# x of one half folded into two accumulators mid-pair; weights' low parts on VectorE at the change of pairs; the opening's last chunk in a scores bank

## The chip, the cores and the metric

The kernel runs on one core of one Trainium2 chip. The metric is the time of one execution on the device, in microseconds (us); of several executions the median is taken. Beside the plain runs there is one profiled execution, whose trace gives the start and length of every instruction on the core's engines: TensorE (PE, with its weight loads PEld), VectorE (DVE), ScalarE (ACT), GpSimd (POOL), and SyncE's queue (SP), which issues nearly all transfers.

## What is computed

One transformer block with adaptive layer norm: sliding attention over a cache, and a gated feed-forward part. Cut to what matters:

```python
mod = (_silu(c) @ w_mod).reshape(c.shape[0], 6, 1, -1)
sa, ca, ga, sb, cb, gb = ...
h = _layernorm(x) * (1 + ca) + sa
x = x + ga * attention(h, k_cache, v_cache, wq, wo)   # 32 query heads, 16 kv heads, Dh 128, last 512 keys
h = _layernorm(x) * (1 + cb) + sb
g, u = h @ w_gate, h @ w_up                           # 576 -> 4608
x = x + gb * ((sigmoid(g) * u) @ w_down)              # 4608 -> 576
```

S = 2048 rows, D = 576, F = 4608, all in float32. The result is x.

## The kernel before

The 2048 rows are four **blocks** of 512 (NB = 4), of four tiles of 128. A float32 product is made of three matmuls on a high and a low part of each operand (`three`): the high part is a rounded copy that ScalarE makes, the low part is the difference, which VectorE or GpSimd makes.

**The opening and the attention.** Blocks 0 and 1 are normalised first. Their normalised rows are transposed in five chunks of channels (NC = 4 whole ones, and the tail as the fifth, k = 4) into the operand hTm (tail: hTt); `ln_shifted` reads a chunk's PSUM bank twice, ScalarE for the high part and then VectorE for the low part. For block 1 `chunks1` does this between the first steps of attention (chunks 0 and 1 in one step, 2, 3 and 4 in the next): even chunks in a bank of the tag ot (two banks, one of which holds the running sum of P times V), odd ones in the only bank wo. Scores and the transposes of exp(scores) take turns in four banks of the tag st. The next step's projections of q (qp<-hTm) follow on TensorE.

**The feed-forward part** uses Strassen's scheme (Winograd's form, seven products in place of eight) twice: blocks are taken in **pairs** (0: blocks 0 and 1; 1: blocks 2 and 3). The loop `for u in range(U + 1)` goes through 72 **units**, one group of 128 hidden channels each: NF = 36 for pair 0 (u = 0 to 35), 36 for pair 1. A unit has seven `product`s of seven matmuls in the banks a (two), b and c; the last of a unit, A22, runs in the next unit, behind that unit's A11. v1 is the running value that takes the last sum from a bank a (DVE v<-a,v) before A22 may add to that bank.

In a product's course `downs` places one or two steps of the second matmul (`down_some`: three matmuls into one of four banks w, and an addition on VectorE to an accumulator, x<-w,x). The downs of two units are queued in `todo`, 28 for each such group, sorted by accumulator (`ORDER`: A11, S3, A22, S1, A12, S2, S4; four tiles each). In the last group of a pair they are sorted by tile. The accumulators and x22 lie in the tiles x0 to x3 (x_101 to x_104 in the order listings): A11 and S3 in x0, A22 and S1 in x1, A12 and S2 in x2, S4 and x22 in x3.

**The end of a pair.** A22, A12 and S4 begin as x of the block (loaded by `init_acc` from the scratch xscr); for S1's quarter of the output x is loaded into x22 by itself. When the last downs of a pair are done for a tile, `finish` queues the additions that make the four output quarters: four on VectorE, four on GpSimd (S4 += S1, S1 += x22, S4 += S2, S1 += S3). `finish_some` takes one from each engine's list at each down and two at each product; `outs_some` stores a finished quarter once the product counter `made` has reached its due number: one product later for VectorE's, three later for GpSimd's. Then `init_acc` loads the accumulators for pair 1: A22 in unit 38, A12 and S4 in unit 39. All of this runs in the first units of pair 1 (36 to 39), beside its products.

**Weights.** `load_w` loads a product's first weights into sr (four buffers), `split_w` makes of them sw (six buffers): ScalarE the high part, and for the low part sw<-sr,sw, GpSimd and VectorE take turns (`turn`). So weights are split several products ahead, and a load waits for the low part four loads before it.

**Order.** Each engine works through its instructions in one order and stops at one that has to wait; SP's queue does likewise, so a store that waits for GpSimd holds up every load behind it. The order comes from a scheduling layer (`tc`); what is written with `pin` stays in program order among its like, the rest may be moved by it.

Of the kernel before, what the change touches and what calls it, by code (L numbers as in the profile page):

```python
# [44 lines left out]
def adaln_block_kernel(ctx: ExitStack, tc: tile.TileContext, x, k_cache, v_cache, wq, wo, w_gate, w_up, w_down,  # L45
# [36 lines left out]
    def ps_pt():  # L82
        return psum("st", 4, [P, BLK])
# [4 lines left out]
    def ps_ot():  # L88
        return psum("ot", 2, [P, BLK])

    def ps_wide():
        return psum("wo", 1, [P, BLK])
# [7 lines left out]
    def f32(ap):  # L100
        return ap.bitcast(F32)
# [10 lines left out]
    def pin(i):  # L112
        if not early[0]:
            tc.keep_in_program_order(i)
# [309 lines left out]
    def chunks1(ks):  # L424
        if 0 in ks:
            new_hT(1)
        for k in ks:
            p = ps_wide() if k % 2 else ps_ot()
            for t in range(TPB):
                ln_channels(1, t, k, p)  # L430
            ln_shifted(1, k, p)
# [707 lines left out]
            SR[u, a] = t  # L1139
            at_use[0] += 1  # L1140

    turn = [0]

    def split_w():
        if not SR:
            return
        u, a = next(iter(SR))
        r = SR.pop((u, a))
        t = fpool["s"].tile([P, 5, P], F32R, tag="sw", name="sw", bufs=6)
        nc.scalar.activation(t[:, 0:3], r, AF.Copy)  # L1150
        turn[0] += 1
        (nc.gpsimd if turn[0] % 2 else nc.vector).tensor_sub(t[:, 3:5], r[:, 0:2], f32(t[:, 0:2]))
        SW[u, a] = t

    ORDER = (A11, S3, A22, S1, A12, S2, S4)
# [52 lines left out]
    def finish(pair, a, t):  # L1208
        def add(eng, to, by, ends=()):
            fin[eng is nc.gpsimd].append((eng, ACC[to][:, t, :], by, [(e, pair, t) for e in ends if pair == 0]))  # L1210

        c = {k: ACC[k][:, t, :] for k in ORDER}
        if a == A11:
            add(nc.vector, A12, c[A11])
            add(nc.vector, S2, c[A11])
        if a == S2:
            add(nc.vector, S3, c[S2])
            add(nc.vector, A22, c[S3], (A22, A12))
            add(nc.gpsimd, S4, c[S1])
            add(nc.gpsimd, S1, x22[:, t, :])  # L1220
            add(nc.gpsimd, S4, c[S2], (S4,))
            add(nc.gpsimd, S1, c[S3], (S1,))

    def finish_some(k):
        for _ in range(k):
            for some in fin:
                if some:
                    eng, to, by, ends = some.pop(0)
                    pin(eng.tensor_add(to, to, by))
                    q = eng is nc.gpsimd  # L1230
                    outs[q].extend((made[0] + 1 + 2 * q,) + e for e in ends)

    def outs_some(k, forced=()):
        for q, some in enumerate(outs):
# [55 lines left out]
    def product(u, a, c, p, first, downs=(2, 5)):  # L1290
        w, h = SW.pop((u, a)), HC[c]
        pairs = []
        for s in range(2):
            pairs.append((w[:, s, :], h[:, 3 + s, :]))
            pairs.append((w[:, 3 + s, :], h[:, s, :]))
            pairs.append((w[:, s, :], h[:, s, :]))
        pairs.append((w[:, 2, :], h[:, 2, :]))
        for n, (l, r) in enumerate(pairs):
            m = nc.tensor.matmul(p, l, r, start=first and n == 0, stop=n == len(pairs) - 1, skip_group_check=not first)
            if u == 0 and a != A22:  # L1300
                pin(m)
            if n in downs:
                down_some(1)
        split_w()
        load_w()
        made[0] += 1
        if not todo:
            finish_some(2)
        outs_some(2)
# [113 lines left out]
    for u in range(U + 1):  # L1423
        pair = u // NF
        nxt = (u + 1) // NF if (u + 1) % NF == 0 and u + 1 < U else None
        if u == NF + 3:
            assert not any(fin), fin
            outs_some(0, (0, 1))
        if u in (3, NF + 3):
            init_acc(pair, slice(1, 3))  # L1430
        if u in (3, 8, 13, 18):
            late_load((u - 3) // 5)
        if u in (4, 9, 14, 19):
            late_tile((u - 4) // 5)
        if u in (6, 11, 16, 21):
            late_put((u - 6) // 5)
        if u == 3:
            ln_some(HB, True, 0, 13, True)
        if u == NF - 2:
            stage(1, 0)  # L1440
        if u in (NF - 2, U - 4):
            pin(nc.sync.dma_start(x22, xscr[2 * pair + 1][:, :, D2:]))
        if u == 1:
            split_w()
            load_w()
        downs = (1, 3, 5) if u in (NF + 1, U - 1) else (2, 5)

        def swap(c, to):
            if to:
                load_combo(to, c)  # L1450
                for k in CORDER[CORDER.index(c) + 2 :][:1]:
                    stage(to, k)


        def ahead(c):
            if u == 0:
                load_combo(0, c, True)

        def others(t):
            if u in (1, 2):  # L1460
                ln_stats(HB + u - 1, t, True)

        if u < U:
            pa, pb, pc = fpsum("a", 2, [P, BLK]), fpsum("b", 1, [P, BLK]), fpsum("c", 1, [P, BLK])
            if nxt:
                stage(nxt, T1)
            product(u, A11, B11, pa, True, downs)
            nc.scalar.activation(pb, pa, AF.Copy)
            swap(B11, nxt)
            ahead(B21)  # L1470
            others(0)
        if u > 0:
            v, qa = back
            g = (u - 1) // 2
            if u == U:
                down_some(len(todo))
                finish_some(8)
                assert not any(fin)
            product(u - 1, A22, T4, qa, False, downs if u < U else ())
            swap(T4, pair if u % NF == 0 and u < U else None)  # L1480
            nc.vector.tensor_mul(v, qa, v)
            if g == GL:
                a = A11 if u % 2 else A12
                VAL[g, a] = v
                split_val(g, a, lo=nc.vector)
            elif u % 2:
                VAL[g, A11] = v
                split_val(g, A11)
                sum_val(g, S3, "-", A11, A21)
                later = (g, S3)  # L1490
            else:
                VAL[g, A12] = v
                lo = nc.vector if g == GL - 1 else nc.gpsimd
                split_val(g, A12, lo=lo)
                split_val(g, S2, lo=lo)
                sum_val(g, S4, "-", A12, S2)
                if g % NG == NG - 1 or g == GL - 1:
                    split_val(g, S4)
                    todo += [(g, a, t) for a in ORDER[:2] for t in range(TPB)]
                    todo += [(g, a, t) for t in range(TPB) for a in (A22, S1, A12, S4, S2)]  # L1500
                else:
                    later = (g, S4)
                    todo += [(g, a, t) for a in ORDER for t in range(TPB)]
        if u == 2:
            init_acc(pair, slice(0, 1))
        if u == U:
            last_downs()
            break
        product(u, S1, T1, pc, True, downs)
        if u == NF + 2:  # L1510
            assert not fin[0], fin
            outs_some(0, (0,))
            init_acc(pair, slice(0, 1))
        swap(T1, nxt)
        ahead(T2)
        others(1)
        v1 = keep(pc, "v1", 2)
        product(u, A12, B21, pb, False, downs)
        swap(B21, nxt)
        ahead(B22)  # L1520
        others(2)
        g0 = val("g0", 3)
        pin(nc.scalar.activation(g0, pb, AF.Sigmoid))
        product(u, S2, T2, pa, False, downs)
        swap(T2, nxt)
        ahead(T3)
        g1 = keep(pa, "g1", 1)
        product(u, S4, B22, pc, False, downs)
        swap(B22, nxt)
        ahead(T4)  # L1530
        nc.vector.tensor_add(g1, pc, g1)
        pin(nc.scalar.activation(g1, g1, AF.Sigmoid))
        others(3)
        if later is not None:
            split_val(*later, True)
            later = None
        product(u, S3, T3, pa, False, downs)
        swap(T3, nxt)
        nc.vector.tensor_add(v1, pa, v1)
        nc.vector.tensor_mul(v1, v1, g1)  # L1540
        g = u // 2
        if g == GL:
            a = A22 if u % 2 else A21
            VAL[g, a] = v1
            split_val(g, a, lo=nc.vector)
        elif u % 2 == 0:
            VAL[g, A21] = v1
        else:
            VAL[g, A22] = v1
            split_val(g, A22)  # L1550
            sum_val(g, S1, "+", A21, A22)
            split_val(g, S1)
            sum_val(g, S2, "-", S1, A11)
        back = g0, pa
# [28 lines left out]
```

## Time and profile before

| what | us |
|---|---|
| median of 3 runs | 3037.52 (3034.82 to 3039.16) |
| profiled execution | 3039.51 |
| its span, first to last instruction | 3037.6 |
| TensorE busy | 3012.5 |
| VectorE busy | 2088.5 |
| ScalarE busy | 1696.8 |
| GpSimd busy | 1659.7 |

The attention takes the first 1400 us of the span, its output projection follows, and the feed-forward part runs from some 1784 us to the end; the units at the change of pairs (36 to 39) lie between 2394 and 2468. A row of the timeline is: start, length of the group, engine, line, operation, out<-in, shape, count, and in brackets how long the engine had been idle before it and who ended that. All engine work of this kernel is recorded under one line (L36, a helper), so the tile names tell the operations apart. A row of a table by windows is: stretch, its length, then busy time and count of PE, PEld, DVE, ACT and POOL, the granted TensorE clock (1.00 is full), the DMA engines' busy share and GB/s.

### The profile page before, as it was taken

Reading aid. Unit: us, or ns where it says so; the run is one execution under the profiler, and the core shown is the slowest. Engines: PE = TensorE matmul, PEld = TensorE weight load, DVE = VectorE, ACT = ScalarE, POOL = GpSimd, SP = SyncE. Lnnn points to the kernel's source line nnn. Section 1 sums busy time; section 2 is a strip of 40 time slices with the busy share of each in tenths; the row PEclk is TensorE's granted clock in tenths of the full one; section 3 lists DMA queues with packets and bytes.
Section 4 is the critical chain, followed back from the end, with each engine's and each line's share of the span. In section 5 each row is a group of like instructions: output and inputs, shape, how many; then the busy total and the mean of one; then the engine's idle time right before and its main releaser. Section 6 shows DMA issues by size and latency. Waiting matters only on the chain.

```text
span 3037.6 us, 49150 instructions
## 1 busy us (share of the span) xinstructions
PE 3012.5 (99%) x16644; PEld 2593.6 (85%) x16644; DVE 2088.5 (69%) x3686; ACT 1696.8 (56%) x3424; POOL 1659.7 (55%) x1549
## 2 busy tenths in 40 slices
PE   8999999999999999999999999999999999999999
PEld 6888888888888888888999988888888878888888
DVE  6666666677666666667888877666666856666667
ACT  5666666657666676555444654444444544444443
POOL 2344457634577887412555026667655666655664
PEclk9999999999999999999999999999999999999999
DMA  4677777776777777775548656555655565555553
GB/s 126 185 197 215 198 223 227 227 207 186 207 233 236 244 242 247 210 211 176 207 154 315 237 164 187 165 146 159 184 143 142 156 189 138 146 146 143 140 151 112
DMA packets 485788, 571.32 MB, mean 188 GB/s; under 512 B 52000, under 2 KB 434208, under 8 KB 476832
## 3 DMA queue, kind: packets, MB, share of 16 engines
q1 hardware_dynamic: 484400, 567.65, 63.1%
q8 instruction: 132, 2.16, 0.3%
q14 instruction: 120, 0.98, 0.1%
q10 hardware_dynamic: 1136, 0.53, 0.1%
HBM read 394.33 MB, written 173.70 MB: 187 GB/s over the span
## 4 chain that ended last, share of the span: by engine, by line
PE 92%; DVE 2%; POOL 2%; issue 1%; DMA 1%; ACT 1%; SPq 0%; POOLq 0%; ACTq 0%; DVEq 0%
PE a L36 21%; PE st L36 18%; PE w L36 13%; PE qp L36 13%; PE ot L36 11%; PE c L36 10%; PE b L36 5%; POOL x L36 1%; DVE x L36 1%; PE wo L36 0%; SPq L36 0%; DMA vt<-sscr 0%; ACT pp L36 0%; DVE ptt L36 0%; POOL vs L36 0%
## 5 line engine op out<-in xcount | busy, mean ns | idle before, releaser
L36 DVE TENSOR_TENSOR x<-w,x 128x288 f32<-128x288 f32 x964 | 421.9, 452 | 254.8 <-PE w L36 250.9
L36 PE MATMUL a<-hc,sw 128*128 128x512 f32 x2016 | 585.3, 396 | 5.2 <-DVE v L36 5.2
L36 DVE TENSOR_REDUCE neg<-st 128x1 f32<-128x512 f32 x512 | 352.6, 689 | 276.2 <-PE st L36 275.4
L36 ACT ACTIVATE ptt<-st 128x512 fp32r<-128x512 f32 x512 | 306.4, 598 | 390.8 <-PE st L36 390.0
L36 PE MATMUL ot<-ptt,vs 128*128 128x512 f32 x1536 | 483.0, 422 | 1.7 <-DVE ptt L36 1.6
L36 PE MATMUL st<-kt,qt 128*128 128x512 f32 x1536 | 444.1, 395 | 0.4 <-ACT pp L36 0.4
L36 PE MATMUL qp<-hTm,wa 128*128 128x512 f32 x1524 | 441.3, 398 | 2.3 <-DVE hTm L36 1.2
L36 DVE TENSOR_TENSOR ptt<-st,ptt 128x512 fp32r<-128x512 f32 x512 | 352.0, 688 | 126.9 <-ACT ptt L36 126.7
L36 PEld LDWEIGHTS a<-hc,sw 128*128 128x128 f32 x2016 | 356.7, 189 | 46.2 <-DVE v L36 7.2
L36 ACT ACTIVATE pp<-st,neg 128x512 f32<-128x512 f32 x512 | 350.9, 685 | 43.9 <-DVE neg L36 42.8
L36 POOL TENSOR_TENSOR sw<-sr,sw 128x256 fp32r<-128x256 f32 x252 | 206.4, 820 | 292.4 <-ACT sw L36 291.7
L36 ACT ACTIVATE sw<-sr 128x384 fp32r<-128x384 f32 x504 | 257.8, 519 | 190.2 <-issue 91.5
L36 PEld LDWEIGHTS st<-kt,qt 128*128 128x128 f32 x1536 | 287.2, 188 | 67.5 <-ACT pp L36 1.1
L36 PEld LDWEIGHTS w<-wh,hl 128*128 128x128 f32 x1776 | 298.0, 188 | 53.7 <-DVE x L36 4.4
L36 PEld LDWEIGHTS qp<-hTm,wa 128*128 128x128 f32 x1524 | 281.5, 188 | 69.9 <-DVE qt L36 7.1
L36 PE MATMUL w<-wh,hl 128*128 128x288 f32 x1776 | 328.6, 296 | 1.5 <-DVE x L36 1.5
L36 PEld LDWEIGHTS st<-ident,pp 128*128 128x128 f32 x2048 | 254.7, 140 | 70.7 <-ACT pp L36 0.8
L36 POOL TENSOR_TENSOR x<-x 128x256 f32<-128x256 f32 (+3 forms) x334 | 248.5, 764 | 118.5 <-DMA x<-in_B_w_up_dram 60.5
L36 PE MATMUL st<-ident,pp 128*128 128x128 f32 x2048 | 307.2, 272 | 0.5 <-DVE ptt L36 0.3
L36 PE MATMUL c<-hc,sw 128*128 128x512 f32 x1008 | 303.5, 394 | 0.0
L36 DVE TENSOR_TENSOR sw<-sr,sw 128x256 fp32r<-128x256 f32 x252 | 181.7, 721 | 143.3 <-ACT sw L36 114.5
L36 PEld LDWEIGHTS ot<-ptt,vs 128*128 128x128 f32 x1536 | 252.6, 190 | 30.8 <-DVE ptt L36 4.1
(235 smaller groups left out, 5043.6 us busy)
## 6 DMA issues: line engine op xcount, KB each, us to landing
sr<-wsc SPq DMA_DIRECT2D x504, 192.0 KB
wh<-dsc SPq DMA_DIRECT2D x144, 288.0 KB
dsc<-x SPq DMA_DIRECT2D x34, 1008.0 KB
vr<-oscr SPq DMA_DIRECT2D x32, 1024.0 KB
rb<-rscr SPq DMA_DIRECT2D x126, 256.0 KB
wsc<-x SPq DMA_DIRECT2D x36, 896.0 KB
oscr<-ov SPq DMA_DIRECT2D x63, 512.0 KB
wosc<-x SPq DMA_DIRECT2D x32, 1008.0 KB
```

Of the source, the lines that this page charges most:

```text
L36: i = got(*args, **kw)
```

## The change

```diff
@@ chunks1
-            p = ps_wide() if k % 2 else ps_ot()
+            p = ps_pt() if k == NC else ps_wide() if k % 2 else ps_ot()
@@ split_w
-    turn = [0]
+    turn, busy = [0], [False]
...
-        (nc.gpsimd if turn[0] % 2 else nc.vector).tensor_sub(t[:, 3:5], r[:, 0:2], f32(t[:, 0:2]))
+        (nc.gpsimd if turn[0] % 2 and not busy[0] else nc.vector).tensor_sub(t[:, 3:5], r[:, 0:2], f32(t[:, 0:2]))
@@ finish
             add(nc.gpsimd, S4, c[S1])
-            add(nc.gpsimd, S1, x22[:, t, :])
             add(nc.gpsimd, S4, c[S2], (S4,))
             add(nc.gpsimd, S1, c[S3], (S1,))
@@ finish_some
-                    outs[q].extend((made[0] + 1 + 2 * q,) + e for e in ends)
+                    outs[q].extend((made[0] + 1 + 4 * q,) + e for e in ends)
@@ the loop over units
+        busy[0] = u in (NF + 1, NF + 2)
...
-        if u in (NF - 2, U - 4):
+        if u in (5, NF + 5):
             pin(nc.sync.dma_start(x22, xscr[2 * pair + 1][:, :, D2:]))
...
+        def fold(t):
+            if u % NF in (9, 10):
+                a, op = ((ACC[S4], nc.gpsimd.tensor_sub), (ACC[S1], nc.gpsimd.tensor_add))[u % 2]
+                pin(op(a[:, t, :], a[:, t, :], x22[:, t, :]))
...
         product(u, A12, B21, pb, False, downs)
+        fold(0)
...
         product(u, S2, T2, pa, False, downs)
+        fold(1)
...
         product(u, S4, B22, pc, False, downs)
+        fold(2)
...
         product(u, S3, T3, pa, False, downs)
+        fold(3)
```

The last chunk of block 1's opening takes a bank of the tag st. x22 is added to S1 in units 9 and 45 (four tiles each, on GpSimd), and, since S1 is added to S4 at the pair's end, taken off S4 in units 10 and 46; the four additions of x22 at the end of each pair go. x22 is loaded in units 5 and 41 in place of 34 and 68. In units 37 and 38 every low part of weights is VectorE's. GpSimd's stores become due five products later in place of three.

Three places show how this moves instructions. **The opening**, TensorE, the step in which chunks 2, 3 and 4 of block 1 are transposed (h and extra are normalised rows, extra their tail):

```order
 L36 MATMUL ot<-ident,h 128x128 x4
 L36 MATMUL wo<-ident,h 128x128 x4
-L36 MATMUL ot<-ident,extra 128x128 x4
+L36 MATMUL st<-ident,extra 128x128 x4
 L36 MATMUL qp<-hTm,wa 128x512 x7
 L36 MATMUL st<-kt,qt 128x512 x3
```

The order stays; only the bank of chunk 4 is another.

**VectorE at the end of unit 37**, up to the addition of bank a to v1 (v<-a,v) and the product behind it. x_101<-x_101,x_103 and x_102<-x_102,x_101 are the finishing additions, x<-w the downs, sw<-sr,sw the low parts. Before:

```order
L36 TENSOR_TENSOR x_101<-x_101,x_103 128x288
L36 TENSOR_TENSOR x_104<-w,x_104 128x288
L36 TENSOR_TENSOR x_102<-x_102,x_101 128x288
L36 TENSOR_TENSOR x_103<-w,x_103 128x288
L36 TENSOR_TENSOR g_27190<-c,g_27190 128x512
L36 TENSOR_TENSOR sw<-sr,sw 128x256
L36 TENSOR_TENSOR x_101<-x_101,x_103 128x288
L36 TENSOR_TENSOR v_27118<-a,v_27118 128x512
L36 TENSOR_TENSOR v_27118<-v_27118,g_27190 128x512
L36 TENSOR_TENSOR x_102<-x_102,x_101 128x288
```

Now:

```order
L36 TENSOR_TENSOR x_102<-x_102,x_101 128x288
L36 TENSOR_TENSOR x_103<-w,x_103 128x288
L36 TENSOR_TENSOR sw<-sr,sw 128x256
L36 TENSOR_TENSOR x_104<-w,x_104 128x288
L36 TENSOR_TENSOR x_103<-w,x_103 128x288
L36 TENSOR_TENSOR g_27198<-c,g_27198 128x512
L36 TENSOR_TENSOR x_101<-x_101,x_103 128x288
L36 TENSOR_TENSOR sw<-sr,sw 128x256
L36 TENSOR_TENSOR x_102<-x_102,x_101 128x288
L36 TENSOR_TENSOR v_27126<-a,v_27126 128x512
L36 TENSOR_TENSOR sw<-sr,sw 128x256
L36 TENSOR_TENSOR v_27126<-v_27126,g_27198 128x512
```

More low parts stand among the same operations (three more ahead of v<-a,v, counted from the unit's start), and the last finishing addition, which followed v<-v,g, now stands ahead of v<-a,v.

**SP's queue and GpSimd behind it**, in unit 38, up to the load of A22's accumulator (x_102<-xscr). SP before:

```order
L36 DMA out_dram<-x_104 128x288
L36 DMA sr<-wsc_303 128x384
L36 DMA out_dram<-x_102 128x288 x2
L36 DMA out_dram<-x_103 128x288
L36 DMA out_dram<-x_104 128x288
L36 DMA sr<-wsc_303 128x384 x2
L36 DMA out_dram<-x_102 128x288
L36 DMA x_102<-xscr_299 128x4x288
```

SP now:

```order
L36 DMA out_dram<-x_102 128x288
L36 DMA sr<-wsc_303 128x384
L36 DMA out_dram<-x_102 128x288
L36 DMA out_dram<-x_103 128x288
L36 DMA out_dram<-x_104 128x288
L36 DMA sr<-wsc_303 128x384
L36 DMA out_dram<-x_102 128x288
L36 DMA sr<-wsc_303 128x384
L36 DMA x_102<-xscr_299 128x4x288
```

The last store, of S1's last tile, stands ahead of the accumulator's load in both; one weight load has moved behind it. The addition that this store waits for is the last x1_102<-x1_102,x0_101 on GpSimd. Before:

```order
L36 TENSOR_TENSOR vs_27257<-v1_26908,v1_27118 128x512
L36 TENSOR_TENSOR x1_102<-x1_102,x3_104 128x288
L36 TENSOR_TENSOR hl_27254<-v1_27118,hl_27254 128x512
L36 TENSOR_TENSOR vs_27262<-vs_27257,g0_26936 128x512
L36 TENSOR_TENSOR hl_27259<-vs_27257,hl_27259 128x512
L36 TENSOR_TENSOR x3_104<-x3_104,x2_103 128x288
L36 TENSOR_TENSOR sw_27326<-sr_27226,sw_27326 128x256
L36 TENSOR_TENSOR vs_27306<-g0_27152,vs_27262 128x512
L36 TENSOR_TENSOR hl_27300<-g0_27152,hl_27300 128x512
L36 TENSOR_TENSOR x1_102<-x1_102,x0_101 128x288
```

Now:

```order
L36 TENSOR_TENSOR x3_104<-x3_104,x1_102 128x288
L36 TENSOR_TENSOR x3_104<-x3_104,x2_103 128x288
L36 TENSOR_TENSOR vs_27266<-v1_26916,v1_27126 128x512
L36 TENSOR_TENSOR vs_27271<-vs_27266,g0_26944 128x512
L36 TENSOR_TENSOR hl_27263<-v1_27126,hl_27263 128x512
L36 TENSOR_TENSOR hl_27268<-vs_27266,hl_27268 128x512
L36 TENSOR_TENSOR x1_102<-x1_102,x0_101 128x288
```

Four operations stand between the finished v1 and that addition, where there were nine.

## The prediction

> **What bounds the kernel now.** I read the page's busy shares first, then the waits of TensorE, and only then the timeline at each place where TensorE stood still.
>
> ```profile
> PE 3012.5 (99%) x16644; PEld 2593.6 (85%) x16644; DVE 2088.5 (69%) x3686; ACT 1696.8 (56%) x3424; POOL 1659.7 (55%) x1549
> PE a L36 <- DVE v L36: 5.2, 6, 3.0
> PE w L36 <- DVE x L36: 2.2, 4, 0.7
> PE ot L36 <- DVE hTm L36: 1.9, 1, 1.9
> ```
>
> TensorE is busy 3012.5 us of a span of 3037.6, and no matmul is added or taken away. So only its standstills (and the half clock that can follow one) can be won: 25.1 us in all, of which these three rows are the ones that the change touches. Each row reads: who waited for whom, microseconds in all, times, longest.
>
> The first place is the opening.
>
> ```profile
> 51.91 0.60 PE L36 MATMUL wo<-ident,h 128*128 128x128 f32 x4
> 54.43 0.66 PE L36 MATMUL ot<-ident,extra 128*128 128x128 f32 x4 [1.92 <-DVE hTm L36]
> 54.84 2.65 PE L36 MATMUL qp<-hTm,wa 128*128 128x512 f32 x7
> 59.95 1.31 PE L36 MATMUL qp<-hTm,wa 128*128 128x512 f32 x5
> 53.62 0.75 DVE L36 SCALAR_TENSOR_TENSOR hTm<-ot,csb,hTm 128x512 fp32r<-128x512 f32 x1 [0.89 <-ACT hTm L36]
> 56.00:58.00 2.00, 2.00 (x6) 1.60 (x5) 0.59 (x1) 0.00 (x0) 0.00 (x0) 0.50 0.79 168
> 63.38 0.86 PE L36 MATMUL qp<-hTm,wa 128*128 128x512 f32 x3
> 64.07 0.85 PE L36 MATMUL st<-kt,qt 128*128 128x512 f32 x3
> 64.77 0.60 PE L36 MATMUL st<-ident,pp 128*128 128x128 f32 x4
> 65.12 0.94 PE L36 MATMUL ot<-ptt,vs 128*128 128x512 f32 x3
> 65.90 1.08 PE L36 MATMUL qp<-hTm,wa 128*128 128x512 f32 x4
> ```
>
> Chunk 4's transposes wait 1.92 us until VectorE has read chunk 2 out of the same bank (53.62 + 0.75 = 54.37), and behind that idle time the granted clock is 0.50 (the column after POOL's). From 51.91 to 59.95 TensorE needs 8.04 us. The last five rows give the same kinds of work at full speed by the distance of their starts: 0.69 for three qp, 0.70 for three scores, 0.35 for four transposes, 0.78 for three ot. What stands between 51.91 and 59.95 is two groups of four transposes (0.70), seven qp (1.61), three scores (0.70), four transposes (0.35) and three ot (0.78): 4.14 us. The place costs 3.9 us, half of it clock.
>
> The second place is the change of pairs.
>
> ```profile
> 2434.62 1.90 PE L36 MATMUL a<-hc,sw 128*128 128x512 f32 x7 [0.29 <-DVE v L36]
> 2442.74 0.66 PE L36 MATMUL w<-wh,hl 128*128 128x288 f32 x3 [0.69 <-DVE x L36]
> 2446.19 0.66 PE L36 MATMUL w<-wh,hl 128*128 128x288 f32 x3 [0.56 <-DVE x L36]
> 2452.62 0.39 PE L36 MATMUL a<-hc,sw 128*128 128x512 f32 x1
> 2456.02 1.65 PE L36 MATMUL a<-hc,sw 128*128 128x512 f32 x3 [3.01 <-DVE v L36]
> 2463.70 0.86 PE L36 MATMUL b<-hc,sw 128*128 128x512 f32 x3
> 2466.12 0.85 PE L36 MATMUL a<-hc,sw 128*128 128x512 f32 x3
> 2458.00:2462.00 4.00, 4.00 (x13) 3.32 (x13) 2.10 (x5) 0.94 (x2) 0.51 (x2) 0.50 1.08 364
> 2454.55 0.82 DVE L36 TENSOR_TENSOR x<-w,x 128x288 f32<-128x288 f32 x2 [3.32 <-DMA x<-xscr]
> 2439.32 6.52 SPq L36 DMA_DIRECT2D out_dram<-x  x4
> 2449.64 0.34 SPq L36 DMA_DIRECT2D out_dram<-x  x1
> 2450.07 0.53 SPq L36 DMA_DIRECT2D x<-xscr  x1
> 2448.81 0.81 POOL L36 TENSOR_TENSOR x<-x,x 128x288 f32<-128x288 f32 x1
> ```
>
> Read it backwards. TensorE stands 3.01 us until VectorE has added a to v1; VectorE stood 3.32 us before that for the load of A22's accumulator; that load was issued at 2450.07, behind stores in SP's queue (four of them held it for 6.52 us), the last of which could go at 2449.64, when GpSimd's last add (2448.81 + 0.81) was done. A product with two downs takes 2466.12 - 2463.70 = 2.42 us; from 2452.62 to 2463.70 stand one matmul (0.24) and two such products, 5.08 us, in 11.08. So this standstill and its half clock cost 6.0 us, and with 0.29, 0.69 and 0.56 the place costs 7.5. GpSimd's backlog is its root.
>
> **The change, part by part.** *Chunk 4 in a scores bank.* Same transposes, same two reads. The bank taken is the one of scores 7, read long before. Left is that the seventh qp needs chunk 2's low part, ready at 54.37 as before: 51.91 + 0.70 + six qp (1.38) = 53.99, so 0.4 us is still waited, too short by the rows above (0.69 without a clock drop) to halve anything. Gain 3.9 - 0.4 = **3.5 us**; bounds 0 (the wait moves to the qp, with its clock) and 3.9. The four banks rotate on, and one step later they are used as before.
>
> *The fold.* At the change, and again at the kernel's end, 12 GpSimd adds remain of 16: four of 0.81 saved, 3.2 us. In exchange there are eight adds in each of pairs 0 and 1, in units 9, 10 and 45, 46. I cost them at nothing: GpSimd's fullest such stretch is unit 9, which also has a late tile.
>
> ```profile
> 1938.00:1955.00 17.00, 17.00 (x93) 14.88 (x92) 10.42 (x21) 7.83 (x16) 14.08 (x14) 1.00 0.47 131
> ```
>
> 14.08 + 4 x 0.81 = 17.3 of 17.0 us: 0.3 us late, which unit 10 takes up; the first low part of hl that is late by it is multiplied in the next unit at the earliest. If that cover fails, the fold is the slower rival below. The x22 load moves from units 34 and 68 to 5 and 41, past other loads of SP's queue. It is as large as the accumulator's:
>
> ```profile
> x<-xscr SPq DMA_DIRECT2D x3, 576.0 KB
> ```
>
> That one landed 4.5 us after its issue (2450.07 to 2454.55), and x22 is read four units after its new place, each of 17 us; the weight loads behind it can lose those few microseconds out of the six products, 2.42 us each, for which weights lie split ahead. I cost it at 0, and at 2 x 1.9 if a stall like the opening's came of it.
>
> *Low parts on VectorE.* In units 37 and 38 GpSimd loses seven, VectorE gains seven. Three of them stand before the v1 add of unit 37, and one finishing add has moved ahead of it too.
>
> ```profile
> 2421.40 1.29 POOL L36 TENSOR_TENSOR vs<-g,v 128x512 f32<-128x512 f32 x1 [1.36 <-DVE g L36]
> 2421.61 1.36 DVE L36 TENSOR_TENSOR sw<-sr,sw 128x256 fp32r<-128x256 f32 x1
> 2461.46 0.41 DVE L36 TENSOR_TENSOR sw<-sr,sw 128x256 fp32r<-128x256 f32 x1
> 2429.18 0.46 DVE L36 TENSOR_TENSOR x<-w,x 128x288 f32<-128x288 f32 x1 [0.54 <-PE w L36]
> 2432.91 1.06 DVE L36 TENSOR_TENSOR x<-x,x 128x288 f32<-128x288 f32 x1
> 2433.89 0.68 DVE L36 TENSOR_TENSOR v<-a,v 128x512 f32<-128x512 f32 x1
> 2438.73 1.28 POOL L36 TENSOR_TENSOR vs<-v,v 128x512 f32<-128x512 f32 x1
> 2418.00:2434.00 16.00, 16.00 (x89) 13.95 (x87) 15.46 (x31) 6.29 (x12) 14.54 (x16) 1.00 0.44 132
> ```
>
> A low part takes 0.41 us beside an idle GpSimd, and 1.36 when it meets one of its operations (here it ended when vs had ended, plus its own time). So the four extra operations cost between 4 x 0.41 = 1.6 and 3 x 1.36 + 1.06 = 5.1 us of VectorE; of this its only idle time in the unit, 0.54, comes off. What also comes off is relief: of GpSimd's 14.54 us in the 16 before the wait (the last row; the column after VectorE's and ScalarE's), three low parts and three adds go, some 6 x 0.81 = 4.9, so a third. VectorE's other operations on SBUF meet it less often: one meeting fewer is worth 1.36 - 0.41, and I count one, 1 us, as an estimate. I take 2.5 for the four (nearer the short end, since GpSimd's queue now runs dry before the unit's end): v1 is 1.0 us late, and TensorE's 0.29 there becomes 1.3. In return GpSimd's adds: vs can start once v1 is there, at some 2437.5 instead of 2438.73, and four operations of 1.26 stand between it and the last add, which now ends near 2443.3 instead of 2449.62. SP's store and the accumulator's load follow near 2444; landed in 4.5 us as before, it is there at 2448.5, and VectorE asks for it at about 2450.5. The 3.01 and its half clock are gone, and the two waits of VectorE for weights behind the same queue (0.69, 0.56) with them; I leave 0.3 for those. Gain 7.5 - 1.3 - 0.3 = **5.9 us**; bounds 0 and 7.5. The later due numbers of GpSimd's stores only keep them out of SP's way: nothing reads them.
>
> [...]
>
> *The end.* Four adds fewer on GpSimd beside the last two units:
>
> ```profile
> 3010.82 0.67 PE L36 MATMUL w<-wgate,hl 128*128 128x288 f32 x3 [0.70 <-DVE x L36]
> 3020.41 1.90 PE L36 MATMUL a<-hc,sw 128*128 128x512 f32 x7 [0.51 <-DVE v L36]
> ```
>
> At most 1.2 us; one finishing add also moved ahead of the v1 add there (0.4 at least). I take **0.5**.
>
> **Sum.** 3.5 + 5.9 + 0.5 = 9.9. The profiled execution took 3039.51 us, 1.9 more than its span and 2.0 more than the median; its span would become 3027.7, and the median 3037.5 - 9.9 = 3027.6: I forecast **3028 us**, own range 3024.5 to 3031.
>
> **Rivals.** 1. *The late v1 halves the clock.* The four extras meet GpSimd at the long end (5.1 - 0.54 - 1 = 3.6 late, or anything above about 1.5): an idle time of 1.92 did halve the clock, one of 0.70 did not. Middle case: a stall of 2.4 and 1.7 us of half clock (the opening's 3.9 less its own 1.92 and 0.3), gain 9.9 - 2.8 = 7.1: 3030.5. For it: VectorE had 0.54 us to spare in the unit. Against: GpSimd is less full there. [...]
> 2. *Nothing stays:* relief pays for all, the stalls go whole: 3.9 + 7.5 + 1.2 = 12.6, 3025.
> 3. *The opening's wait moves* to the qp behind it: gain 6.4, 3031.
> 4. *The accumulator's load stays late:* SP's queue still stands, now for low parts on VectorE (a weight load waits for the low part four before it): the 6.0 remain, gain about 4, 3033.5. Against: VectorE was idle more than half of 2438 to 2456.
> 5. *Slower: the fold.* Each of its four units makes GpSimd late enough that TensorE waits for hl, with half clock: 1.9 + 1.7 = 3.6 each as in the opening, 14.4 in all, less 9.9: 3042. It decides from 2.5 us a unit on. Against: 0.3 late against a unit of slack.
>
> **How the numbers follow.** Forecast 0.49, rivals 0.18, 0.13, 0.07, 0.07, 0.06. A measurement of this kernel tells 0.2% (6.1 us) from no change. Faster by more: 0.48 of the forecast's, 0.13 of rival 1, all of 2, half of 3: 0.77. Slower: 0.06. The rest, 0.17, within. The range leaves out rival 5 and the tails: 3023.5 to 3035.
>
> **What would show it.** Right: st<-ident,extra with no wait near 52.5 and full clock to 60; the load x<-xscr at the change issued near 2440 (the opening's gain shifts all by 3.5), before VectorE asks; the one wait left there is a on v, near 1.3 us. Wrong: clock 0.50 behind that wait (rival 1), VectorE on x<-xscr (4), TensorE's w on GpSimd's hl in units 10, 11, 46 or 47 (5), qp on hTm for over 1 us (3).

## The result, and the profile after

| | before | after |
|---|---|---|
| median | 3037.18 us (3034.79 to 3039.16, 8 runs) | 3028.30 us (3027.62 to 3029.94, 8 runs) |
| profiled execution | 3039.51 us | 3027.62 us |
| its span | 3037.6 us | 3025.8 us |

The ratio is 0.9971, its 95% interval 0.9961 to 0.9982: 8.9 us less by the medians. The two profiled executions differ by 11.9, since that of before lies 2.3 above its median and that of after 0.7 below.

The busy shares and TensorE's waits, as shown of before:

```profile
PE 3006.9 (99%) x16644; PEld 2591.7 (86%) x16644; DVE 2091.2 (69%) x3693; ACT 1695.2 (56%) x3424; POOL 1658.5 (55%) x1550
PE a L36 <- DVE v L36: 1.6, 4, 0.6
PE w L36 <- DVE x L36: 1.3, 3, 0.8
```

The row `ot<-ident,extra` waiting for hTm is gone, a waits 1.6 us for v instead of 5.2, w 1.3 for x instead of 2.2.

The opening, timeline of TensorE, and the clock behind it in the table by windows:

```profile
51.93 0.60 PE L36 MATMUL wo<-ident,h 128*128 128x128 f32 x4
52.37 0.60 PE L36 MATMUL st<-ident,extra 128*128 128x128 f32 x4
52.72 2.22 PE L36 MATMUL qp<-hTm,wa 128*128 128x512 f32 x7
54.78 0.86 PE L36 MATMUL st<-kt,qt 128*128 128x512 f32 x3
56.61 1.30 PE L36 MATMUL qp<-hTm,wa 128*128 128x512 f32 x5
56.00:58.00 2.00, 2.00 (x11) 1.64 (x10) 1.63 (x3) 1.26 (x3) 0.00 (x0) 1.00 0.69 199
```

From the transposes of chunk 3 to the five qp it is 4.68 us, where before it was 8.04 (51.91 to 59.95): 3.36 less. The seven qp take 2.06 to the next scores, 0.45 more than seven at 0.23. That fits the wait for chunk 2's low part that was left: VectorE ended it at 54.38, and at 0.23 each six qp were through at 54.10.

The change of pairs, in the order in which the chain runs (GpSimd's last addition S1 += S3, SP's queue, VectorE, TensorE):

```profile
2439.24 0.99 POOL L36 TENSOR_TENSOR x<-x,x 128x288 f32<-128x288 f32 x1
2440.26 0.33 SPq L36 DMA_DIRECT2D out_dram<-x  x1
2440.68 0.38 SPq L36 DMA_DIRECT2D sr<-wsc  x1
2441.16 0.53 SPq L36 DMA_DIRECT2D x<-xscr  x1
2445.84 0.82 DVE L36 TENSOR_TENSOR x<-w,x 128x288 f32<-128x288 f32 x2 [0.98 <-DMA x<-xscr]
2430.82 1.89 PE L36 MATMUL a<-hc,sw 128*128 128x512 f32 x7 [0.32 <-DVE v L36]
2438.56 0.66 PE L36 MATMUL w<-wh,hl 128*128 128x288 f32 x3 [0.31 <-DVE x L36]
2452.48 0.86 PE L36 MATMUL b<-hc,sw 128*128 128x512 f32 x3
```

The same products stood at 2434.62 and 2463.70 before: 29.08 us between them, now 21.66. So 7.4 us went here. A22's load is issued at 2441.16; VectorE waits 0.98 for it and TensorE not at all, and the clock stays at 1.00. The wait for v1 is 0.32, where it was 0.29.

The end has one wait left of two (2999.79, w for x, 0.79; it was 0.70); the a that waited 0.51 for v starts at once. Matched matmuls (the n-th of one trace against the n-th of the other, by their starts) put the gain at 3.8 to 4.2 us before the change of pairs, 11.2 behind it and 11.8 at the end. TensorE's busy time fell by 5.6 us, from 3012.5 to 3006.9, though it does the same matmuls: most of that is half clock, which counts as busy (behind the first 5 us, before's trace has 13.7 us of it and the change's some 3.4).

### The profile page after: what moved, and what is told of

Same layout as the page of the kernel before. It is cut to its first block, busy times and chain, and to the rows that moved or that the text cites. A ratio compares the mean times of both kernels' runs of the same rounds, so it can differ in the third digit from the quotient of the medians.

```text
span 3025.8 us, 49171 instructions
## 1 busy us (share of the span) xinstructions
PE 3006.9 (99%) x16644; PEld 2591.7 (86%) x16644; DVE 2091.2 (69%) x3693; ACT 1695.2 (56%) x3424; POOL 1658.5 (55%) x1550
## 4 chain that ended last, share of the span: by engine, by line
PE 93%; DVE 3%; POOL 2%; issue 1%; ACT 1%; DMA 1%; SPq 0%; POOLq 0%; DVEq 0%; ACTq 0%
PE a L36 21%; PE st L36 18%; PE qp L36 13%; PE w L36 13%; PE ot L36 11%; PE c L36 11%; PE b L36 5%; POOL x L36 1%; DVE x L36 1%; PE wo L36 0%; DVE sw L36 0%; POOL vs L36 0%; ACT pp L36 0%; DVE ptt L36 0%; POOL hl L36 0%
## 5 line engine op out<-in xcount | busy, mean ns | idle before, releaser
L36 POOL TENSOR_TENSOR sw<-sr,sw 128x256 fp32r<-128x256 f32 x245 | 199.1, 813 | 282.1 <-ACT sw L36 282.1
L36 DVE TENSOR_TENSOR sw<-sr,sw 128x256 fp32r<-128x256 f32 x259 | 189.1, 730 | 140.8 <-ACT sw L36 113.9
```

The source lines that it names most:

```text
L36: i = got(*args, **kw)
```

## The experiments

Each ran beside the kernel before on the same chip (before's medians there: 3037.2 to 3037.4). One table gives what they have in common, times from the profiled execution of each: how long TensorE waited for v1 in unit 37; how long after the start of that addition (v<-a) SP issued A22's load; how long VectorE waited for it; how long TensorE then stood; and the median. The first row is the kernel before, the second the change.

| kernel | v1 | load after v<-a | VectorE waits | TensorE stands | median |
|---|---|---|---|---|---|
| before | 0.29 | 16.18 | 3.32 | 3.01 | 3037.2 |
| the change | 0.32 | 11.08 | 0.98 | 0 | 3028.3 |
| chunk 4's bank undone | 0.32 | 11.09 | 1.40 | 0 | 3031.0 |
| low parts undone | 1.24 | 11.31 | 2.38 | 0.43 | 3029.8 |
| fold undone | 0.46 | 15.04 | 3.42 | 2.01 | 3032.3 |
| before, two lists | 1.11 | 13.91 | 4.62 | 2.33 | 3035.2 |
| fold undone, two lists | 2.09 | 5.13 | 0 | 0 | 3031.8 |
| the change, two lists | 1.09 | 4.83 | 0 | 0 | 3029.1 |
| low parts in unit 38 only | 1.25 | 9.55 | 0 | 0 | 3028.6 |
| before, two lists, five sr | 1.11 | 9.52 | 0 | 0 | 3032.0 |
| the same and chunk 4's bank | 1.13 | 9.39 | 0 | 0 | 3029.3 |

**Chunk 4's bank undone.**

```diff
-            p = ps_pt() if k == NC else ps_wide() if k % 2 else ps_ot()
+            p = ps_wide() if k % 2 else ps_ot()
```

> The change without its opening part: chunk 4 of block 1 in a bank ot again. Theory (the bank is the whole of it): TensorE waits 1.9 us on hTm again, clock 0.50 behind it, and the matched matmuls of 60 us stand 3.3 to 3.5 us later than with the change; 3028.3 + 3.4 = 3031.7 us. Rival (the attention has slack that takes the opening's loss up, or the gain came from elsewhere): 3028.3 to 3029.5.

3031.02 us, ratio to before 0.9981 (0.9973 to 0.9990): 2.7 more than the change. The wait of 1.91 at 54.30 and the half clock behind it are back. The rest of the table's row is nearly that of the change, and matched matmuls lose only 0.2 over the change of pairs, so this part does not lean on the others.

**Low parts undone.**

```diff
-        busy[0] = u in (NF + 1, NF + 2)
```

> The change without the low parts on VectorE: units 37 and 38 take turns again. Theory (what decides is where the last addition S1 += S3 stands in GpSimd's order, since A22's load is queued behind its store): without the low parts of x22's additions it stands ahead of the operations that wait for v1, so it ends near 2434.5 in this kernel's clock and the load is issued before 2437, in time; nothing is lost, 3028.3 us within 1. Rival (the prediction's: GpSimd's backlog, three low parts of about 0.9 more, sets the load): the load 2.7 us later, past VectorE's 0.98 of waiting, a standstill of 1.5 to 2.5 and half clock behind it, 3030.5 to 3032.5.

3029.79 us (0.9976, 0.9967 to 0.9985): between the two. The timelines of SP and GpSimd say why:

```profile
2438.49 0.38 SPq L36 DMA_DIRECT2D out_dram<-x  x1
2442.26 0.33 SPq L36 DMA_DIRECT2D sr<-wsc  x1
2442.68 0.53 SPq L36 DMA_DIRECT2D x<-xscr  x1
2441.50 0.74 POOL L36 TENSOR_TENSOR sw<-sr,sw 128x256 fp32r<-128x256 f32 x1
```

The last store of S1 left at 2438.49, as the theory had it, and still A22's load was late: between them stands a weight load, and that waits until GpSimd has made the low part four loads before it (2441.50 + 0.74 = 2442.24). So SP's queue is held by GpSimd in two ways, by a store and by a weight load. By matched matmuls A22's load costs 0.7, of which 0.43 is the standstill. That v1 comes late (1.24 instead of 0.32) costs nothing net over the change of pairs; the run with unit 38 alone shows why. The rest of the 1.5 between the medians is not traced.

**Fold undone.**

```diff
+            add(nc.gpsimd, S1, x22[:, t, :])
...
-        if u in (5, NF + 5):
+        if u in (NF - 2, U - 4):
...
-            if u % NF in (9, 10):
+            if False:
```

> The change without the fold: x22 is loaded and added at the pair's end as before, units 9, 10, 45, 46 have no fold. Theory (place in GpSimd's order): the last S1 += S3 stands again behind six operations that need v1 or g0, ends about 4 to 5 us later than 2440.23, the load lands about 3 to 4 us after VectorE asks: standstill of 1 to 3 us, with half clock at the upper end, 3030 to 3034 us. Rival (the low parts on VectorE are what relieves GpSimd): 3028.3 within 1. Rival of the fold's cost: if units 9, 10, 45 and 46 lose time by the fold, this kernel wins it back there.

3032.26 us (0.9986, 0.9977 to 0.9995), 4.0 more than the change. Here no weight load ahead of A22's waits for GpSimd, but the last S1 += S3 stands behind six operations that need v1 or g0 (timelines of GpSimd, SP and TensorE):

```profile
2444.05 0.99 POOL L36 TENSOR_TENSOR x<-x,x 128x288 f32<-128x288 f32 x1
2445.49 0.53 SPq L36 DMA_DIRECT2D x<-xscr  x1
2440.21 0.66 PE L36 MATMUL w<-wh,hl 128*128 128x288 f32 x3 [1.59 <-DVE x L36]
2451.46 0.97 PE L36 MATMUL a<-hc,sw 128*128 128x512 f32 x3 [2.01 <-DVE v L36]
```

**Two lists in the kernel before.** In `finish` and `finish_some` the comparison `eng is nc.gpsimd` is never true: the wrapper around nc makes a new object each time. So the finishing additions stand in one list, one of them comes out at each down, and each store is due one product later, whatever its engine. The description ahead of the prediction follows the program's text, not this. It also means that the change's new due number (4 * q in place of 2 * q) does nothing, since q is 0 in both.

```diff
-            fin[eng is nc.gpsimd].append(...)
+            fin[eng._of is nc.gpsimd._of].append(...)
...
-                    q = eng is nc.gpsimd
+                    q = eng._of is nc.gpsimd._of
```

> The kernel before, with one thing mended: the comparison of engines in finish and finish_some compares a fresh wrapper with a fresh wrapper and is never true, so all finishing additions stand in one list and come out one at a time; here there are two lists, as the text of the program means. GpSimd has as many operations as before. Theory (place in GpSimd's order): the last S1 += S3 moves ahead of the operations that need v1, ends near 2439.5 instead of 2449.6, the load lands before VectorE asks, the 3.01 and the half clock go: gain 5 to 7, 3030 to 3032 us. Rival (GpSimd's amount of work sets it, or its later hl make TensorE wait instead): gain under 2, 3035.5 or more.

3035.24 us (0.9996, 0.9987 to 1.0005), against 3030 to 3032 expected: this theory fell, by the other half of the same queue (SP and GpSimd):

```profile
2440.83 4.85 SPq L36 DMA_DIRECT2D sr<-wsc  x2
2445.73 0.42 SPq L36 DMA_DIRECT2D out_dram<-x  x1
2446.20 0.53 SPq L36 DMA_DIRECT2D x<-xscr  x1
2444.58 0.74 POOL L36 TENSOR_TENSOR sw<-sr,sw 128x256 fp32r<-128x256 f32 x1
```

The additions were done by 2437.21, but two weight loads held the queue until GpSimd's low part of 2444.58 was there (2445.32).

**Two lists with the low parts on VectorE, without the fold.** The edit of two lists on the kernel with the fold undone.

> The change without its fold (GpSimd keeps all 16 finishing additions), but with one list of them for each engine. Theory, as the runs so far leave it: A22's load stands behind whatever in SP's queue waits for GpSimd, be it the store of the last S1 or a weight load that waits for GpSimd's low part; here neither is left ahead of it (low parts on VectorE, the last stores queued behind the load), so it is issued by 2441 and TensorE does not stand for it: 3028.3 to 3029.5 us without any fold. Rival (GpSimd's amount of work decides, so the four additions have to go): load at 2444 or later, 3031 to 3032.5 like the kernel without the fold.

3031.81 us (0.9982, 0.9973 to 0.9990). Neither theory had it: A22's load went out at 2438.13 and nobody waited for it, yet the time is that of the rival. TensorE stood for v1 instead:

```profile
2433.74 1.89 PE L36 MATMUL a<-hc,sw 128*128 128x512 f32 x7 [2.09 <-DVE v L36]
```

GpSimd's four additions matter after all, and VectorE is where they show: GpSimd is busy 15.21 of the 16 us ahead of v1, and VectorE's finishing additions there take 917 ns each, against 681 in the change. The wait for v1 is 1.8 longer than in the change, and matched matmuls lose 1.5 over the whole change of pairs, of the 3.5 us by which this kernel's median lies over the change's; its own profiled execution, at 3030.57, is faster than its median. What the other executions lose stays open.

**The whole change with two lists.** The same edit on the change.

> The whole change with one list of finishing additions for each engine. Theory: A22's load comes earlier than 2441.16, VectorE's 0.98 us of waiting for it goes, and none of it reaches TensorE, which did not stand for it: 3028.3 us within 0.7. Rival: what is left of the wait is on the path, 3027 to 3027.5; or the additions that now stand ahead of v1 make it later: 3029 or more.

3029.14 us (0.9973, 0.9962 to 0.9984), just past the theory's bound: the load comes 6 us earlier and wins nothing. The wait for v1 is 0.77 longer, which is what the second rival feared, but matched matmuls lose only 0.5 over the change of pairs and win 0.3 back at the end. The difference of 0.8 is smaller than the spread of either kernel (1.9 and 2.3), so it is not shown to be a loss.

**Low parts on VectorE in unit 38 alone.**

```diff
-        busy[0] = u in (NF + 1, NF + 2)
+        busy[0] = u == NF + 2
```

> The change with the low parts on VectorE in unit 38 alone; unit 37 takes turns. Theory: the weight loads just ahead of A22's load wait for unit 38's low parts, so it is issued by 2440.5 (2442.68 where GpSimd makes some of them) and the 0.43 of standstill there goes; v1 in unit 37 stays late as there (1.24), 3029.2 us. Rival (unit 37's low parts hold the queue too): load at 2442 or later, 3029.8 us. The times are too near; the trace decides.

3028.58 us (0.9971, 0.9959 to 0.9982), no different from the change. In the trace the load is in time (issued at 2441.88, later than 2440.5 in its clock, but 9.55 after v<-a), so it is unit 38's low parts that free SP's queue. Unit 37's do another thing: without them TensorE waits 1.25 for v1 and not 0.32. VectorE's groups and GpSimd's busy time (the last figure before the clock) over the 16 us ahead of v<-a, first of the change, then of this kernel:

```profile
L36 DVE TENSOR_TENSOR x<-x,x 128x288 f32<-128x288 f32 x8 | 5.4, 681 | 0.0
L36 DVE TENSOR_TENSOR sw<-sr,sw 128x256 fp32r<-128x256 f32 x7 | 5.0, 715 | 0.0
L36 DVE TENSOR_TENSOR x<-w,x 128x288 f32<-128x288 f32 x16 | 6.7, 445 | 0.0
2414.08:2430.08 16.00, 15.90 (x87) 13.65 (x86) 16.00 (x33) 5.67 (x11) 10.69 (x11) 1.00 0.52 154
```

```profile
L36 DVE TENSOR_TENSOR x<-x,x 128x288 f32<-128x288 f32 x8 | 6.9, 861 | 0.0
L36 DVE TENSOR_TENSOR sw<-sr,sw 128x256 fp32r<-128x256 f32 x3 | 3.1, 1049 | 0.0
L36 DVE TENSOR_TENSOR x<-w,x 128x288 f32<-128x288 f32 x15 | 6.4, 444 | 0.2 <-PE w L36 0.2
2416.33:2432.33 16.00, 15.48 (x84) 13.20 (x82) 15.76 (x28) 6.70 (x13) 14.43 (x16) 1.00 0.57 174
```

Four low parts more cost VectorE 1.9 us, and the eight additions beside them get 1.5 cheaper, 681 ns each instead of 861, while GpSimd is busy 10.69 us and not 14.43. VectorE does 33 operations in the time of 28. Its additions x<-w, which read one input from PSUM, take 445 ns in the one and 444 in the other; what is longer here are the two groups with both inputs in SBUF (861 against 681, 1049 against 715). From the v1 of unit 36 to that of unit 37 VectorE needs 18.24 us in the change (2411.84 to 2430.08) and 18.83 here (2413.50 to 2432.33): the moved low parts make v1 0.59 earlier. TensorE has nothing of it. Matched matmuls stand 1.7 us behind the change's both before and behind the change of pairs, because the change loses the same time at two other places, where it waits for VectorE to free a bank w (0.4 at 2423.55 and 0.6 at 2438.56, by matched matmuls). So v1's column of the table is not a loss by itself.

**Five buffers sr.** The kernel before with two lists, and one buffer more, so that the weight load next to A22's waits for VectorE's low part.

```diff
-            t = fpool["s"].tile([P, 3, P], F32, tag="sr", name="sr", bufs=4)
+            t = fpool["s"].tile([P, 3, P], F32, tag="sr", name="sr", bufs=5)
```

> The kernel before with two lists, as run, and with five buffers sr in place of four, so that a weight load waits for the low part five loads before it, which next to A22's load is VectorE's. No operation is moved from GpSimd. Theory (a weight load that waits for GpSimd held A22's load at 2446.20 there): the load is issued 1.5 to 3 us earlier, the standstill of 2.33 falls under 1 and its half clock goes: 3031.5 to 3033.5 us. Rival (GpSimd's work is what counts): 3035.2 within 0.7.

3031.95 us (0.9982, 0.9973 to 0.9991), as the theory had it: the load at 2442.58, no standstill, 3.3 us less than with four. GpSimd has every operation it had (1549). The buffer also moves some loads elsewhere in SP's order, so this is not one wait taken away and nothing else; the trace shows the load in time, though.

**The same with chunk 4's bank.**

> The kernel before with three things only: chunk 4's bank, two lists of finishing additions, five buffers sr. No fold, and no low part moved. Theory (A22's load is then in time as in the run of five buffers, and the opening's loss goes): 3031.95 less 2.7 to 3.4, 3028.5 to 3029.3 us, so as good as the change. Rival (the opening's gain is hidden here, or the load is late again): 3030.5 or more.

3029.28 us (0.9974, 0.9964 to 0.9984). Without the fold and without moving a low part it comes within 1.0 us of the change. By matched matmuls 1.2 us are lost over the change of pairs, where TensorE waits 1.13 for v1 and 0.77 for x, and 0.6 at the end, where the four additions of x22 still stand.

**The fold three times over.**

```diff
-                pin(op(a[:, t, :], a[:, t, :], x22[:, t, :]))
+                for o in (op, nc.gpsimd.tensor_add if u % 2 == 0 else nc.gpsimd.tensor_sub, op):
+                    pin(o(a[:, t, :], a[:, t, :], x22[:, t, :]))
```

> The whole change, with each addition of the fold made three times (added, taken off, added again; in the other unit taken off, added, taken off): GpSimd gets 8 operations of 0.81 more in each of units 9, 10, 45 and 46, 6.5 us a unit. Theory (what hides the fold is a unit of slack between GpSimd's low parts of hl and the downs that read them): GpSimd falls behind by up to some 9 us in units 9 and 10 (16.32 and 13.89 of 17 us busy now, 13 us more), catches up in the next unit, and TensorE stands nowhere: 3028.3 us within 1. Rival (the slower rival of the prediction, a late hl with half clock): 2 to 4 us in at least two of the four units, 3033 or more.

3037.86 us (1.0002, 0.9993 to 1.0011), 9.6 more than the change: the cover named for the fold is not the one that holds. Timelines of ScalarE and TensorE in unit 9, first here, then of the change:

```profile
1954.46 0.63 ACT L36 ACTIVATE hl<-vs 128x512 fp32r<-128x512 f32 x1 [8.04 <-POOL vs L36]
1955.00 0.58 ACT L36 ACTIVATE b<-a 128x512 f32<-128x512 f32 x1
1955.63 1.65 PE L36 MATMUL b<-hc,sw 128*128 128x512 f32 x3 [4.54 <-ACT b L36]
1951.00:1968.00 17.00, 12.46 (x54) 10.66 (x54) 8.58 (x16) 7.57 (x15) 16.77 (x18) 0.80 0.34 92
```

```profile
1947.37 0.58 ACT L36 ACTIVATE b<-a 128x512 f32<-128x512 f32 x1
1949.64 0.86 PE L36 MATMUL b<-hc,sw 128*128 128x512 f32 x3
1934.00:1951.00 17.00, 17.00 (x93) 14.85 (x93) 10.60 (x21) 7.14 (x14) 16.32 (x17) 1.00 0.42 120
```

GpSimd's difference vs is wanted at once, by ScalarE, and behind that high part in ScalarE's queue stands the copy b<-a, from which TensorE's next product in bank b starts. With the fold once, b is there at 1947.95 and taken at 1949.64: 1.7 us to spare, not a unit. Three times, TensorE stands 4.54 us and pays the half clock (0.80 over the unit): unit 9 loses 7.3 us by matched matmuls. In pair 1 the same wait is only 0.78, and the two units there lose 1.7, so the rival's total came (3033 or more), but not its 2 to 4 us in at least two units.

**The same trick on another bank.** The transposes of the second group's keys, which wait 1.87 us for a bank st at 38.98, in the bank wo.

```diff
-        p = ps_pt()
+        p = ps_wide() if gg == 1 else ps_pt()
```

> The whole change, and the same exchange of a bank once more: the transposes of the second group's keys, which wait 1.87 us at 38.98 for a bank st, go into the bank wo, free at that time. Theory (the place is not on the path: the kernels whose clock was not halved there arrive about 1 us earlier and wait 2.6 instead of 1.0 for h at 49.06): the wait of 1.87 shrinks, the wait for h grows by as much, 3028.3 us within 0.8. Rival (each wait with its half clock is lost time): 1.9 to 3.6 less, 3024.7 to 3026.4 us.

3028.91 us (0.9974, 0.9963 to 0.9985), as the theory had it. The wait shrinks to 0.49 and 0.57, and 3.09 us are waited for h at 49.17, where the change had 1.02:

```profile
40.99 0.96 PE L36 MATMUL st<-kt,qt 128*128 128x512 f32 x3 [0.49 <-ACT pp L36]
42.96 0.96 PE L36 MATMUL ot<-ptt,vs 128*128 128x512 f32 x3 [0.57 <-DVE ptt L36]
49.17 0.33 PE L36 MATMUL ot<-ident,h 128*128 128x128 f32 x1 [3.09 <-POOL h L36]
```

No kernel here is faster than the change.

## Why the prediction was right, and where its steps were not

**The number.** 9.9 us were forecast, 8.9 measured by the medians, and 11.9 by the two profiled executions. The terms were made from the profiled execution of before, and that one had the half clock at both places; not every execution has (last section). Of the 76 executions of before beside the experiments 27 have a mean clock of 0.998, as the profiled one has, with a median of 3037.7 us; the other 49 have a higher one and a median of 3036.7. So the sum's agreement with the medians is partly luck: the change of pairs was put too low, and the median has less to lose than the profile. The frame was also too narrow: the 25.1 us of idle time were not all that could be won, since 5.6 of the gain came out of TensorE's busy time, mostly as half clock. The terms themselves did count it.

**The opening, 3.5: right.** 3.36 in the trace, where the half clock followed, and 0.45 left on the seventh qp where 0.4 was said. Undoing it costs 2.7 by the medians. In the profiled execution of before with two lists, which kept its clock behind the same wait of 1.92, the place loses only 1.7 against the change, so 2.7 fits a mixture of the two.

**The change of pairs, 5.9: right in its mechanism, too small by 1.5.** The load left near 2441 as said (2440), SP's queue was what it waited in, and the standstill of 3.01 went with its half clock. Not as said: VectorE still waited 0.98 for it; TensorE had that much to spare. Of the 1.5, 1.0 is the step below. The other 0.5 lies between 2434.62 and 2452.62 of before, a stretch that shrank by 1.40 where 0.95 (0.69 + 0.56 less 0.3) was counted.

**The step that failed is "v1 is 1.0 us late, and TensorE's 0.29 there becomes 1.3".** It stayed at 0.32. From the v1 of unit 36 to that of unit 37 VectorE needed 17.88 us before (2416.01 to 2433.89) and 18.24 now, so v1 is 0.36 late and not 1.0. Its busy time in that stretch went from 17.34 to 18.24: the four extra operations cost 0.9 net, where the prediction had 1.5 (2.5 less 1.0 of relief). TensorE paid the 0.36 earlier in the unit, at the bank w at 2423.55, and not at v1.

What was mis-sized is the relief, taken as one meeting of VectorE with GpSimd fewer. With the low parts undone the stretch takes 18.83: v1 is 0.95 late, which is near the 1.06 priced for the finishing addition that moved ahead of it (eight stand in the stretch, where there were seven). The three low parts then brought it back to 18.24 in place of adding to it, with GpSimd busy 10.69 us of 16 ahead of v1, where it was 14.43 before and with the low parts in unit 38 only. With the fold undone the same low parts leave v1 0.16 later than before (18.04 against 17.88), so they are paid for, or nearly so, in both orders. Rival 1, which priced the same term at the long end, went the wrong way. In the 16 us ahead of v1 one and the same addition on VectorE took 681 ns in the change, with GpSimd busy 10.69 us; 789 before and 861 with the low parts in unit 38 only, both at 14.43; and 917 at 15.21 (two lists without the fold). Over these four the addition is longer where GpSimd is busier, though 14.43 gave two values; so GpSimd's load was a cost of VectorE too, of which the prediction counted too little.

**"GpSimd's backlog is its root": half of it.** The load waited behind two things that need GpSimd, a store and a weight load that waits for a low part. The fold frees the first, the low parts of unit 38 the second. Undoing either brings a late load back (0.43 and 2.01), and a mended list alone leaves most of the standstill (2.33 of 3.01) until the weight load is freed as well. Why the fold moves the last addition so far was not seen either: all additions leave one list, one at each down, so four fewer bring the last one forward in the program and not only in GpSimd's time.

**The fold, 0: right, with the wrong cover.** TensorE is full in unit 9 (17.00 of 17), but the slack is 1.7 us through ScalarE, not a unit. The slower rival had the right price and the wrong waiter.

**Store numbers, 0: right,** but because the edit does nothing, not because it keeps stores out of the way.

**The end, 0.5: right** (0.6 by matched matmuls, from 11.2 to 11.8).

## What to carry to other kernels

A load at the end of an in-order queue is as late as the latest engine that anything ahead of it waits for (here A22's load left at 2450.07 behind a store that GpSimd held to 2449.64, in before, and at 2442.68 behind a weight load held to 2442.26, with the low parts undone): list every wait in that queue, weight loads as well as stores, since freeing one kind alone can win nothing. Where one engine's operations get longer while another is busy (here 861 ns against 681 for the same addition), price a moved operation by what it takes off its new neighbours as well as by its own length, and then see whether the engine that waits is held at another place instead. And check a cover by its first reader on every engine's queue, not by the last use of the data.

## What the runs showed of the hardware

Whether an idle time of TensorE was followed by half clock did not go by its length alone. Three pairs of rows by windows of 3.41 us, each window followed by the next, first two of before, then one of the kernel with the keys' bank (where its windows lie is the author's estimate, since its clock did not drop there):

```profile
38.59:42.00 3.41, 1.53 (x11) 1.20 (x10) 2.00 (x4) 3.21 (x7) 2.06 (x3) 1.00 0.22 23
42.00:45.41 3.41, 3.41 (x11) 2.74 (x11) 2.11 (x4) 2.98 (x7) 3.06 (x4) 0.50 0.57 153
52.24:55.66 3.42, 1.50 (x11) 1.13 (x10) 1.90 (x3) 2.47 (x5) 0.34 (x1) 1.00 0.00 0
55.66:59.07 3.41, 3.41 (x11) 2.62 (x10) 1.01 (x2) 0.15 (x1) 0.00 (x0) 0.50 0.80 195
```

```profile
47.34:50.75 3.41, 1.58 (x11) 1.40 (x12) 1.34 (x3) 2.66 (x7) 1.69 (x2) 1.00 0.06 5
50.75:54.17 3.42, 3.42 (x24) 2.93 (x22) 2.53 (x5) 2.87 (x7) 1.29 (x1) 1.00 0.01 4
```

An idle time of 1.88 halved the clock and one of 3.09 did not. One wait at one place did both: up to 40.88 TensorE waited 1.87 for a bank st in the change, where the clock fell to 0.50 at 41.81, and 1.87 with the fold undone, where it did not fall; the next three scores took 1.48 in the one (42.69) and 0.86 in the other (42.30). In before the clock was half from 42.00 to 45.41, from 55.66 to 59.07 and from 2455.22 to 2462.05: 3.41, 3.41 and 6.83 us, and the second stretch begins 13.66 behind the first, four times 3.41. In the 3.41 us ahead of these three TensorE was busy 1.53, 1.50 and 1.20, and 1.54 ahead of the change's 41.81. In the last two rows the idle time is cut by the window's start at 47.34; there 1.58 was busy and the clock stayed at 1.00. But the kernel before with two lists waited its 1.92 us at the same place of the opening, was busy 1.54 from 50.85 to 54.27, and kept its clock at 1.00 from there to 57.68. So a limit in busy time is not shown. That one wait is followed by half clock in one execution and not in another would fit the spread of before, 4.4 us.

The half clock at 41.81 cost the change nothing: TensorE then waited 1.02 us for h and went on at 49.05; with the fold undone, where the clock did not drop, it waited 2.57 and went on at 49.06.
